# Polynomial-sketch attention and a gated FFN on one core: tokens in 64 rows of 17, sketches in 64x64 tiles, engines ordered by a list schedule

## The chip, the core and the metric

The kernel runs on one core of a Trainium2 chip. The core's engines are TensorE (PE in the profile; its weight loads are PEld), VectorE (DVE), ScalarE (ACT), GpSimd (POOL) and SyncE (SP), each with its own queue of instructions that it works through in order, and 16 DMA engines. The metric is the time of one execution on the device in microseconds; lower is better.

## What is computed

Four batches of four heads with 1088 tokens each and a head size of 32; the sketch size R is 8; the FFN takes 4352 tokens of width 128 (four heads side by side) through 1536 hidden columns.

```python
def phi(x):
    a = np.einsum('rd,bhsd->bhsr', S1, x)
    b = np.einsum('rd,bhsd->bhsr', S2, x)
    return np.einsum('bhsi,bhsj->bhsij', a, b).reshape(*x.shape[:-1], r * r)
q_p, k_p = (phi(q), phi(k))
kv = np.einsum('bhsf,bhsd->bhfd', k_p, v)
z = np.sum(k_p, axis=2)
num = np.einsum('bhsf,bhfd->bhsd', q_p, kv)
den = np.einsum('bhsf,bhf->bhs', q_p, z)[..., None] + 1e-06
attn = num / den
x = attn.transpose(0, 2, 1, 3).reshape(B * S, H * D)
out = np.maximum(x @ w_gate, 0.0) * (x @ w_val) @ w_out
```

A token of a head has 64 features, the outer product of its two sketches. Keys of a whole batch must be summed before a query of that batch can be finished.

## The kernel before, in words

**Tiling of tokens.** Of a batch's 1088 tokens the first 1024 lie as 128 partitions of 8 tokens (C = 8), in tiles k_sb, q_sb and v_sb with four heads along the free axis (load_main). The last 64 tokens of all four batches form a fifth group: kr, qr and vr, 32 partitions per batch with 2 tokens each (load_rest).

**Keys of a batch (class K).** t1 turns 32x32 blocks on VectorE (kt), so that the head dimension lies on the partitions, four heads at once. ab multiplies by the sketch matrix sk in fp32 on TensorE, 128 rows by 128 columns, 512 columns at a time. t2 turns the result back (abk). phi makes the outer products (kp) on POOL, for batch 0 half of them on VectorE. kvz sums kp times v and the sketches' products for z in one PSUM bank, four fp16 and one fp32 product per column of tokens, and then adds the leftover rows (abr, kpr, vr) with 32-row products. evac masks the sums into zd and kv_bd. w multiplies zd with s1rep and VectorE writes the result into wst, the matrix that queries are multiplied with; it yields both sketches and the denominator's factor.

**Queries (class Q).** Work goes in groups of n token columns: t1 (VectorE), ab (fp32 on TensorE, one product per head), t2 (VectorE), den (product on POOL or VectorE, sum and reciprocal on VectorE, scaling), phi (outer product qp), tr (2n transposes on TensorE), tre (copy to SBUF on ScalarE), num (two products with 64 columns each, one for each half of PSUM's partitions) and x (cast to xT on ScalarE). The groups are 2, 2 and 4 columns of batch 0, two of 4 for each other batch and 2 columns of leftover rows.

**FFN (class F).** 102 units, each of 512 columns: g (L414), Relu on ScalarE (L416), v (L419), product with v on VectorE to ht (L421), and four 128-column products of ht with wo into o_ps (L430), which gathers a group's output. The last unit of a group evicts o_ps on ScalarE (L437) and SyncE writes it out (L440, L447).

**Order.** manual_schedule keeps the written order on each engine. The head (L473 to L522) is written out by hand, with warm(n) putting n small products on zeros into TensorE's queue (L155, 111 in all). After it, at(slot, ...) puts attention steps into the loop over units (L565): keys some 46 to 11 units ahead of the batch's second group, queries 14 to 1.5 units ahead of their own. A unit's out comes LAG = 3 units behind its g and v, and 5 for a group's first.

**PSUM.** Two banks for g, three for v, one for o, two ("m") for all attention products. SBUF: four g_sb, eight ht.

**DMA.** SyncE issues k and q of each batch and the leftover rows; ScalarE issues S1, S2 and the leftover v; POOL issues v with a cast to fp16 and the three weight matrices, also with a cast.

Of the kernel before, what the change touches and what calls it, by code (L numbers as in the profile page):

```python
# [19 lines left out]
EPS = 1e-6  # L20


@with_exitstack
def kernel(
# [20 lines left out]
    C = S // 128  # L45
    SM = C * 128
    E = (S - SM) // 32
    GC = C // 2
    GT = GC * 128
    RT = E * 128  # L50
    LAG = 3
    HOLD = 2
    assert (B, H, D, R, S - SM) == (4, 4, 32, 8, 64)
# [4 lines left out]
    a_t = ctx.enter_context(tc.tile_pool(name="a_t", bufs=3))  # L58
    a_ab = ctx.enter_context(tc.tile_pool(name="a_ab", bufs=2))
    a_kp = ctx.enter_context(tc.tile_pool(name="a_kp", bufs=2))  # L60
    a_sm = ctx.enter_context(tc.tile_pool(name="a_sm", bufs=2))
    f_g = ctx.enter_context(tc.tile_pool(name="f_g", bufs=4))
    f_h = ctx.enter_context(tc.tile_pool(name="f_h", bufs=8))
    f_o = ctx.enter_context(tc.tile_pool(name="f_o", bufs=2))
    ps_g = ctx.enter_context(tc.tile_pool(name="ps_g", bufs=2, space=bass.MemoryType.PSUM))
    ps_v = ctx.enter_context(tc.tile_pool(name="ps_v", bufs=3, space=bass.MemoryType.PSUM))
    ps_o = ctx.enter_context(tc.tile_pool(name="ps_o", bufs=1, space=bass.MemoryType.PSUM))
    ps_m = ctx.enter_context(tc.tile_pool(name="ps_m", bufs=2, space=bass.MemoryType.PSUM))

    banks = {"m": ps_m, "g": ps_g, "v": ps_v}  # L70

    def bank(x="m"):
        return banks[x].tile([128, 512], FP32, name=f"{x}_ps")


    s16 = const.tile([2 * R, 4, D], FP32, name="s16")
    s1rep = const.tile([128, 4, D], FP32, name="s1rep")
    kr = const.tile([128, H, E * D], FP32, name="kr")
    qr = const.tile([128, H, E * D], FP32, name="qr")
    vr32 = const.tile([128, H, E * D], FP32, name="vr32")  # L80
    vr = const.tile([128, H, E * D], FP16, name="vr")
    k_sb = [const.tile([128, H, C * D], FP32, name=f"k_sb{b}") for b in range(B)]
    q_sb = [const.tile([128, H, C * D], FP32, name=f"q_sb{b}") for b in range(B)]
    v_sb = [const.tile([128, H, C * D], FP16, name=f"v_sb{b}") for b in range(B)]
# [4 lines left out]
    def load_main(eng, dst, src, b):  # L89
        eng.dma_start(out=dst, in_=src[b, :, 0:SM, :].rearrange("h (p c) d -> p h (c d)", c=C))  # L90

    def load_rest(eng, dst, src):
        for b in range(B):
            eng.dma_start(
                out=dst[32 * b:32 * b + 32],
                in_=src[b, :, SM:, :].rearrange("h (t e) d -> t h (e d)", e=E),
            )
# [3 lines left out]
    load_main(nc.sync, k_sb[0], k, 0)  # L101
    load_main(nc.gpsimd, v_sb[0], v, 0)
    load_rest(nc.sync, kr, k)
    load_rest(nc.scalar, vr32, v)
    load_main(nc.sync, q_sb[0], q, 0)
    for b in range(1, B):
        load_main(nc.sync, k_sb[b], k, b)
        load_main(nc.sync, q_sb[b], q, b)
    load_rest(nc.sync, qr, q)

# [3 lines left out]
    scr = const.tile([1, 1], FP16, name="scr")  # L114
    id32 = const.tile([2 * R, 2 * R], FP32, name="id32")
# [3 lines left out]
    nc.gpsimd.dma_start(out=wg, in_=moe_w_gate.rearrange("m (j f) -> m j f", j=NJ))  # L119
    nc.gpsimd.dma_start(out=wv, in_=moe_w_val.rearrange("m (j f) -> m j f", j=NJ))  # L120
    nc.gpsimd.dma_start(out=wo, in_=moe_w_out.rearrange("(j f) m -> f j m", f=128))
# [3 lines left out]
    maskz = const.tile([128, 2, H, R], FP32, name="maskz")  # L125
    nc.gpsimd.memset(maskz, 1.0)
    nc.gpsimd.affine_select(out=maskz, in_=maskz, compare_op=ALU.is_ge, fill=0.0, base=0,
                            pattern=[[-16, 2], [-32, H], [0, R]], channel_multiplier=1)
    nc.gpsimd.affine_select(out=maskz, in_=maskz, compare_op=ALU.is_ge, fill=0.0, base=R - 1,
                            pattern=[[16, 2], [32, H], [0, R]], channel_multiplier=-1)  # L130
    load_main(nc.gpsimd, v_sb[1], v, 1)
    mask = const.tile([128, 4], FP32, name="mask")
    maskw = const.tile([128, 4], FP32, name="maskw")
    maskkv = const.tile([128, 2, D], FP32, name="maskkv")
    sk = const.tile([128, 2, 4, 2, 2 * R], FP32, name="sk")
    wst = [const.tile([128, H, 4, 32], FP32, name=f"wst{b}") for b in range(B + 1)]
    bw = [const.tile([128, GC * H, R + 1], FP32, name=f"bw{i}") for i in range(2)]
    nc.vector.memset(mask, 0.0)
    nc.vector.memset(maskw, 0.0)
    nc.vector.memset(maskkv, 0.0)  # L140
    nc.vector.memset(sk, 0.0)
    for p in range(4):
        nc.vector.memset(mask[32 * p:32 * p + 32, p:p + 1], 1.0)
        nc.vector.memset(maskw[32 * p:32 * p + 32, p:p + 1], DSCALE)
# [3 lines left out]
    for i in range(2):  # L148
        nc.vector.memset(bw[i][:, :, R], EPS * DSCALE)

    def warm(n):

        ps = bank("v")
        for _ in range(n):
            nc.tensor.matmul(ps[:, 0:128], zero, zero, start=True, stop=True)  # L155

    nc.scalar.activation(out=scr, in_=zero[0:1, 0:1], func=ACTF.Relu)
    warm(42)
    st_ps = bank()
    nc.tensor.transpose(st_ps[:, 0:2 * R], s16.rearrange("f p d -> f (p d)"), id32)  # L160
    s_t = const.tile([128, 2 * R], FP32, name="s_t")
    nc.vector.tensor_copy(out=s_t, in_=st_ps[:, 0:2 * R])
    s1_ps = bank()
    nc.tensor.matmul(s1_ps[:, 0:128], sel.rearrange("r x f -> r (x f)"),
                     s16.rearrange("f p d -> f (p d)"), start=True, stop=True)
    nc.scalar.copy(out=s1rep.rearrange("p a d -> p (a d)"), in_=s1_ps[:, 0:128])
    warm(9)

    def fill_static(eng, w):
        eng.tensor_tensor(  # L170
            out=w[:, :, :, 0:2 * R],
            in0=s_t[:, None, None, :].to_broadcast([128, H, 4, 2 * R]),
            in1=mask[:, None, :, None].to_broadcast([128, H, 4, 2 * R]),
            op=ALU.mult,
        )

    for hf in range(2):
        nc.vector.tensor_tensor(
            out=sk[:, hf, :, hf, :],
            in0=s_t[:, None, :].to_broadcast([128, 4, 2 * R]),  # L180
            in1=mask[:, :, None].to_broadcast([128, 4, 2 * R]),
            op=ALU.mult,
        )


    kv_bd = [const.tile([128, 2, 2 * D], FP16, name=f"kv_bd{b}") for b in range(B)]
    xT = const.tile([HD, B * SM + RT], FP16, name="xT")
    abr = const.tile([128, E * H, 32], FP32, name="abr")
    kpr = const.tile([128, E * H, R * R], FP16, name="kpr")

    def outer(eng, dst, ab, a0, b0, n, a=None):

        a_src = ab[:, :, a0:a0 + R] if a is None else a
        eng.tensor_tensor(  # L194
            out=dst.rearrange("s x (i j) -> s x i j", i=R),
            in0=a_src[:, :, :, None].to_broadcast([128, n, R, R]),
            in1=ab[:, :, None, b0:b0 + R].to_broadcast([128, n, R, R]),
            op=ALU.mult,
        )

    def rest_k():
        kt = a_t.tile([128, E * H * 32], FP32, name="ktr")
        nc.vector.transpose(kt, kr.rearrange("p h (e d) -> p e h d", e=E))
        ps = bank("g")
        nc.tensor.matmul(ps[:, 0:E * H * 32], sk[:, 0].rearrange("p a b f -> p (a b f)"), kt,
                         start=True, stop=True)
        nc.vector.transpose(abr.rearrange("p x f -> p (x f)"), ps[:, 0:E * H * 32])
        outer(nc.gpsimd, kpr, abr, 0, R, E * H)

    class K:  # L210


        def __init__(self, b):
            self.b = b

        def t1(self, lo, n):

            if lo == 0:
                self.kt = a_t.tile([128, C, H, 32], FP32, name="kt")
            nc.vector.transpose(  # L220
                self.kt[:, lo:lo + n],
                k_sb[self.b][:, :, lo * D:(lo + n) * D].rearrange("p h (c d) -> p c h d", d=D))

        def ab(self, lo=0, n=GC, x="m"):

            self.ps = bank(x)
            for hf in range(2):
                nc.tensor.matmul(  # L228
                    self.ps[:, 0:n * 128], sk[:, hf].rearrange("p a b f -> p (a b f)"),
                    self.kt[:, hf * GC + lo:hf * GC + lo + n].rearrange("p c h t -> p (c h t)"),  # L230
                    start=(hf == 0), stop=(hf == 1))
# [13 lines left out]
        def kvz(self, lo=0, n=GC, rest=True, x="m"):  # L245
            b = self.b
            if lo == 0:
                self.m = bank(x)
# [20 lines left out]
            if not rest:  # L269
                return  # L270
# [309 lines left out]
    for u in pend:  # L580
        u.out()
# [31 lines left out]
```

## Time and profile before

| What | Value |
|---|---|
| Median of 3 runs | 136.78 us (135.47 to 140.0) |
| Span of the profiled execution | 133.8 us, 2942 instructions |
| The profiled execution's own time on the device | not given beside its span; the runs lie 1.7 to 6.2 us above the span, the median 3.0 |
| Busy: TensorE, VectorE, ScalarE, POOL | 116.8, 98.1, 76.8, 51.4 us |
| Mean granted TensorE clock | 0.995 |
| First g of the FFN; last product of TensorE | 22.69 us; ends at 129.2 us |
| Product to ht, Relu, fp32 key sketch of 512 columns (mean of one record) | 676, 602, 606 ns |
| HBM read and written | 9.05 and 2.23 MB |

How to read it: the span runs from the first to the last instruction of the execution. A row of the timeline gives start, duration, engine, line, operation, output and inputs, shapes, and how many instructions are joined in it. An fp32 product appears as two records. Durations of TensorE's products overlap, so the distance of two starts tells what one costs; the chain of waits goes back from the last instruction to whatever released each step.

### The profile page before, as it was taken

The page shows a single profiled execution, that of the slowest core. Times are in us where ns is not written, and L with a number is a line of the kernel's source. Part 1 is how long each engine was busy: PE and PEld are TensorE (multiplying, and loading weights), DVE is VectorE, ACT ScalarE, POOL GpSimd, SP SyncE. Part 2 cuts the span into 40 slices and gives each one's busy share as a digit, 9 for nine tenths or more (in the row PEclk, how much of TensorE's full clock was granted, in tenths as well). Part 3 has the DMA queues.
Part 4 walks back from the last instruction along what each step waited for, and adds up shares of the span by engine and source line. Part 5 has one row for each costly group of instructions (what it writes and reads, how often), then busy time and mean ns, then how long its engine had stood idle before and what let it go on. Part 6 is the DMA issues. An engine that isn't in the chain of part 4 may idle for free.

```text
span 133.8 us, 2942 instructions
## 1 busy us (share of the span) xinstructions
PE 116.8 (87%) x1102; PEld 82.8 (62%) x1102; DVE 98.1 (73%) x202; ACT 76.8 (57%) x136; POOL 51.4 (38%) x70
## 2 busy tenths in 40 slices
PE   6995989949989999699799998997999689999850
PEld 6984867739856665377466654765656356756740
DVE  4295578899768956997579649776895696988850
ACT  0311003747646674775576837845767949789930
POOL 6955307999602601980017018910260160050000
PEclk9999999999999999999999999999999999999998
DMA  2999999808501000200011002000200010020021
GB/s 63 255 208 253 270 257 355 235 1 105 91 5 39 0 2 0 78 5 0 0 50 34 0 0 83 5 0 0 77 2 5 15 66 0 0 83 0 0 78 39
DMA packets 11485, 9.23 MB, mean 69 GB/s; under 512 B 3792, under 2 KB 10320, under 8 KB 11472
## 3 DMA queue, kind: packets, MB, share of 16 engines
q1 hardware_dynamic: 6864, 6.69, 16.1%
q0 software_dynamic: 3952, 2.23, 11.8%
q10 hardware_dynamic: 656, 0.14, 0.6%
q8 instruction: 8, 0.13, 0.5%
q14 instruction: 5, 0.04, 0.1%
HBM read 9.05 MB, written 2.23 MB: 84 GB/s over the span
## 4 chain that ended last, share of the span: by engine, by line
PE 53%; DVE 15%; DMA 11%; POOL 7%; issue 6%; ACT 4%; ACTq 1%; DVEq 1%; SPq 0%; POOLq 0%
PE o_ps L430 12%; PE g_ps L414 11%; PE v_ps L419 10%; DMA k_sb<-in_k_dram 7%; DVE ht L421 7%; POOL qp L194 4%; PE m_ps L328 4%; PE m_ps L365 3%; DMA vr<-in_v_dram 3%; ACT g_sb L416 3%; PE m_ps L228 3%; DVE abq L336 2%; PE m_ps L264 2%; PE m_ps L383 2%; DVE kt L220 2%
## 5 line engine op out<-in xcount | busy, mean ns | idle before, releaser
L421 DVE TENSOR_TENSOR ht<-g_sb,v_ps 128x512 f16<-128x512 f16 x102 | 65.5, 676 | 16.9 <-ACT g_sb L416 9.4
L416 ACT ACTIVATE g_sb<-g_ps 128x512 f16<-128x512 f32 x102 | 59.5, 602 | 27.8 <-PE g_ps L414 26.5
L419 PE MATMUL v_ps<-xT,wv 128*128 128x512 f16 (+1 forms) x120 | 38.7, 347 | 4.6 <-DVE ht L421 4.6
L414 PE MATMUL g_ps<-xT,wg 128*128 128x512 f16 (+1 forms) x120 | 38.7, 347 | 1.9 <-ACT g_sb L416 1.8
L430 PEld LDWEIGHTS <-ht 128*128 128x128 f16 x408 | 28.7, 99 | 15.4 <-issue 4.4
L430 PE MATMUL o_ps<-wo,ht 128*128 128x128 f16 x408 | 36.2, 219 | 0.2 <-DVE ht L421 0.2
L343 POOL TENSOR_TENSOR bw<-abq 128x128 f32<-128x128 f32 (+1 forms) x7 | 3.0, 433 | 51.0 <-DVE abq L336 51.0
L194 POOL TENSOR_TENSOR qp<-an,abq 128x1024 f16<-128x1024 f32 (+2 forms) x10 | 16.7, 1669 | 7.4 <-DVE an L350 6.9
L419 PEld LDWEIGHTS <-wv 128*128 128x128 f16 x120 | 11.7, 98 | 7.9 <-issue 6.5
L194 POOL TENSOR_TENSOR kp<-abk 128x512 f16<-128x512 f32 x14 | 15.5, 1138 | 1.6 <-DVE abk L237 1.6
L373 ACT COPY pt<-m_ps 128x1024 f16<-128x1024 f16 (+1 forms) x10 | 8.8, 883 | 10.5 <-PE m_ps L365 10.2
L414 PEld LDWEIGHTS <-wg 128*128 128x128 f16 x120 | 11.2, 98 | 4.7 <-issue 3.0
L155 PE MATMUL v_ps<-zero 128*128 128x128 f16 x111 | 9.7, 255 | 1.1 <-DVE maskkv L140 1.1
L328 PE MATMUL m_ps<-qt,wst 128*128 128x128 f32 (+1 forms) x72 | 9.7, 277 | 0.6 <-DVE wst L300 0.6
L328 PEld LDWEIGHTS m_ps<-qt,wst 128*128 128x128 f32 x72 | 9.1, 192 | 1.4 <-DVE wst L300 0.8
L155 PEld LDWEIGHTS <-zero 128*128 128x128 f16 x111 | 8.6, 118 | 1.5 <-DVE maskkv L140 1.1
L437 ACT ACTIVATE o_sb<-o_ps 128x512 f32<-128x512 f32 (+1 forms) x10 | 5.3, 532 | 4.2 <-PE o_ps L430 4.2
L365 PEld LDWEIGHTS <-qp 128*128 128x128 f16 x68 | 4.4, 98 | 3.2 <-POOL qp L194 1.7
L336 DVE STREAM_TRANSPOSE abq<-m_ps 128x512 f32<-128x512 f32 (+1 forms) x9 | 5.9, 651 | 0.6 <-PE m_ps L328 0.6
L264 PE MATMUL m_ps<-abk 128*128 128x64 f32 x32 | 6.2, 289 | 0.0
L346 DVE TENSOR_REDUCE dn<-bw 128x16 f32<-128x144 f32 (+1 forms) x10 | 2.8, 281 | 4.5 <-POOL bw L343 4.4
L220 DVE STREAM_TRANSPOSE kt<-k_sb 128x512 f32<-128x512 f32 (+1 forms) x10 | 5.6, 576 | 0.6 <-DMA k_sb<-in_k_dram 0.6
(80 smaller groups left out, 100.4 us busy)
## 6 DMA issues: line engine op xcount, KB each, us to landing
k_sb<-in_k_dram SPq DMA_DIRECT2D x4, 512.0 KB, 10.0
q_sb<-in_q_dram SPq DMA_DIRECT2D x4, 512.0 KB, 12.2
out_dram<-o_sb SPq DMA_DIRECT2D x7, 256.0 KB, 2.0
v_sb<-in_v_dram POOLq DMA_DIRECT2D x4, 256.0 KB, 5.2
wg<-in_moe_w_gate_dram POOLq DMA_DIRECT2D x1, 384.0 KB, 6.2
wv<-in_moe_w_val_dram POOLq DMA_DIRECT2D x1, 384.0 KB, 7.7
wo<-in_moe_w_out_dram POOLq DMA_DIRECT2D x1, 384.0 KB, 15.0
out_dram<-o_sb SPq DMA_DIRECT2D x2, 128.0 KB, 1.8
```

What stands on the lines that cost most here:

```text
L155: nc.tensor.matmul(ps[:, 0:128], zero, zero, start=True, stop=True)
L194: eng.tensor_tensor(out=dst.rearrange("s x (i j) -> s x i j", i=R), in0=a_src[:, :, :, None].to_broadcast([128, n, R, R]), in1=ab[:, :, No ...
L264: nc.tensor.matmul(m[:, 128:192].rearrange("f (a h j) -> f a h j", a=2, h=H), ab.rearrange("s h f -> s (h f)"), ab.rearrange("s h (a f) -> ...
L328: nc.tensor.matmul(self.ps[:, h * n * 32:(h + 1) * n * 32], wst[self.b][:, h].rearrange("p a f -> p (a f)"), self.qt[:, :, h, :], start=Tr ...
L336: nc.vector.transpose(self.absb.rearrange("p (c h) f -> p c h f", h=H), self.ps[:, 0:n * 128].rearrange("p (h c t) -> p c h t", h=H, c=n))
L365: nc.tensor.transpose(self.ps[:, p, c], self.qp[:, c * H + 2 * p:c * H + 2 * p + 2].rearrange("s h f -> s (h f)"), ident)
L373: eng.copy(out=self.pt, in_=self.ps)
L414: nc.tensor.matmul(g_ps[:, y * W:(y + 1) * W], wg[:, j], x, start=True, stop=True)
L416: nc.scalar.activation(out=g_sb, in_=g_ps, func=ACTF.Relu)
L419: nc.tensor.matmul(v_ps[:, y * W:(y + 1) * W], wv[:, j], x, start=True, stop=True)
L421: nc.vector.tensor_tensor(out=self.ht, in0=g_sb, in1=v_ps, op=ALU.mult)
L430: nc.tensor.matmul(o[:, s], self.ht[:, y * W + s * 128:y * W + (s + 1) * 128], wo[:, j], start=(j == 0 and s == 0), stop=(j == NJ - 1), sk ...
```

## The change

The kernel body is written anew. What it computes, the FFN units and their number stay.

Tokens: a batch's 1088 tokens are 64 rows of 17. k and q lie with two heads on the partitions (128 = 2 heads x 64 rows) and two pairs of heads along the free axis; v lies as 64 rows of the first nine columns over 64 rows of the last eight. No group of leftover rows is loaded by itself; the ninth columns of all batches form the last query group. k of batch 0 comes in two loads by pair of heads, v of batch 0 over SyncE in fp32 with a cast on ScalarE.

Sketches: each product takes 64 rows (one head) and gives 64 partitions (one half of the columns), in four tiles; the two heads write to two adjoining PSUM banks. z is summed by itself, apart from kv. The numerator is one full-width product for each pair of heads, gathered in one bank.

Order: a plan (class Plan) holds every step with an engine, an assumed occupancy and latency, its dependencies, the banks it takes and frees, and due times worked back from the FFN units' (830 ns apart). At each step it takes, over all engines, the earliest task; among tasks of one engine within 30 ns the one due first. The order of planned starts is the order of issue. The assumed times fix only the order: no times are carried into the program. PSUM is one tile of eight banks: the out bank, up to five for g and v, three for attention once the FFN has started. There are ten g_sb, fourteen ht, four o_sb and five sets of query buffers. Filler products go before a TensorE task up to the first g, to three quarters of the planned gap.

```diff
-        eng.dma_start(out=dst, in_=src[b, :, 0:SM, :].rearrange("h (p c) d -> p h (c d)", c=C))
+    def load_pairs(eng, dst, src, b, hp=None):
+        x = src[b].rearrange("(x y) (t c) d -> (y t) x (c d)", y=2, c=C)
...
+    load_pairs(nc.sync, k_sb[0], k, 0, 0)
+    load_pairs(nc.sync, k_sb[0], k, 0, 1)
+    load_pairs(nc.sync, q_sb[0], q, 0)
+    load_v(nc.sync, v32, 0)
     for b in range(1, B):
+        load_pairs(nc.sync, k_sb[b], k, b)
+        load_pairs(nc.sync, q_sb[b], q, b)
...
+    P = Plan(free={"PE": 1200.0, "ACT": 3000.0, "DVE": 2600.0, "POOL": 3600.0},
+             a_max=3, f_max=5, n_banks=7)
...
+        def ke_ab(t, b, hp, first):
+            for h2 in range(2):
+                for st in range(2):
+                    r = slice(64 * h2, 64 * h2 + 64)
+                    nc.tensor.matmul(
+                        ps[64 * st:64 * st + 64, first.bank + h2, 0:CA * 32],
+                        sk[r, hp].rearrange("p a b f -> p (a b f)"),
+                        kt[b][r, hp, CA * st:CA * st + CA].rearrange("p c t -> p (c t)"),
+                        start=hp == 0, stop=hp == 1, skip_group_check=True)
+
+        first = P.add(f"k{b}ab0", "PE", 650, 900, deps=[K.t1[0], t_sk], banks=2)
...
+        def ke_z(t, b):
+            for c in range(CA):
+                x = c % 2
+                ab = abk[b][:, c].rearrange("p h f -> p (h f)")
+                nc.tensor.matmul(ps[64 * x:64 * x + 64, t.bank, 0:H * R], ab,
+                                 ab.rearrange("p (h f) -> p h f", h=H)[:, :, R:2 * R],
+                                 start=c < 2, stop=c >= CA - 2, skip_group_check=True)
...
+        def ke_kv(t, b, lo, hi, m):
+            for c in range(lo, hi):
+                for hp in range(2):
+                    nc.tensor.matmul(
+                        ps[:, m.bank, hp * 64:hp * 64 + 64], kp[b][:, hp, c],
+                        v_sb[b][:, 2 * hp:2 * hp + 2, c * D:(c + 1) * D],
+                        start=(lo == 0 and c == 0 and hp == 0), stop=c == CA - 1,
+                        skip_group_check=True)
...
+        def qe_ab(t, G):
+            n = G.n
+            for hp in range(2):
+                for h2 in range(2):
+                    r = slice(64 * h2, 64 * h2 + 64)
+                    for st in range(2):
+                        o = ps[64 * st:64 * st + 64, t.bank + h2, hp * n * 32:(hp + 1) * n * 32]
...
+                            nc.tensor.matmul(o, wst[G.bs[0]][r, hp].rearrange("p a f -> p (a f)"),
+                                             G.qt[r, hp, st].rearrange("p c t -> p (c t)"),
...
+                    nc.tensor.matmul(
+                        o, kv_bd[G.bs[0]][:, 2 * hp:2 * hp + 2].rearrange("f a d -> f (a d)"),
+                        G.pt[:, hp].rearrange("f c t -> f (c t)"), start=hp == 0, stop=hp == 1)
...
+    T0, STEP = 13000.0, 830.0
...
+            g = P.add(f"g{u}", "PE", 218, 218 + 170, deps=[G.x], banks=1, kind="f",
+                      emit=lambda t, f=e_mm: f(t, wg), at=land["w"] - 3000.0)
...
+            o = P.add(f"out{u}", "PE", 230, 230 + 170, kind="f",
+                      deps=[mult, last_evict if i == 0 else None, outs[-1] if outs else None],
+                      emit=lambda t, U=U, f=e_out: f(t, U), at=land["w"])
...
+            n = int((t.start - now) * 0.75 / (107.0 if now < 5000.0 else 57.0))
+            for _ in range(n):
+                nc.tensor.matmul(ps[:, OB, 0:128], zero, zero, start=True, stop=True)
```

The first query group's den and phi run on VectorE, those of all others on POOL. Key phi runs on POOL, for batch 0's last five columns on VectorE.

## The prediction

> **What bounds the kernel now.** I read the busy table first, then the timeline of TensorE in steady state, the chain of waits, and the timelines of the head and of the end.
>
> ```profile
> PE 116.8 (87%) x1102; PEld 82.8 (62%) x1102; DVE 98.1 (73%) x202; ACT 76.8 (57%) x136; POOL 51.4 (38%) x70
> PEclk9999999999999999999999999999999999999998
> ```
> TensorE is the fullest engine, at a granted clock of 0.9 to 1.0 in all slices, so pace and not clock is the question. Its busy time has modelled ends; the pace is read from starts. TensorE's rows of the steady stretch, by start and duration:
>
> ```profile
> 73.36 0.38 PE L414 MATMUL g_ps<-xT,wg 128*128 128x512 f16 x1
> 73.58 0.38 PE L419 MATMUL v_ps<-xT,wv 128*128 128x512 f16 x1
> 73.79 0.39 PE L430 MATMUL o_ps<-wo,ht 128*128 128x128 f16 x4
> 74.02 0.38 PE L414 MATMUL g_ps<-xT,wg 128*128 128x512 f16 x1
> 74.23 0.38 PE L419 MATMUL v_ps<-xT,wv 128*128 128x512 f16 x1
> 74.54 0.41 PE L383 MATMUL m_ps<-pt,kv_bd 128*64 128x512 f16 x2
> 74.88 0.40 PE L430 MATMUL o_ps<-wo,ht 128*128 128x128 f16 x4
> ```
> From g at 73.36 to the next g at 74.02 an FFN unit costs TensorE 0.655 us (three times 0.218). VectorE does six products in 3.73 us (0.61 each) and ScalarE two Relus in 1.25 us, so TensorE leads narrowly. 102 units make 66.8 us.
>
> The first g stands at 22.69 us and TensorE ends at 129.2: a stretch of 106.5 us. The attention work in it, by starts: key sketches 2 x 1.77; key sums 3 x 2.2 (1.45 for the main rows, 0.75 with its gap for the leftover rows); the w product 3 x 0.44; query sketches 7 x 0.95 + 0.84; transposes 64 x 0.055; numerators 7 x 0.43 + 0.6. That is 26.0 us. So 66.8 + 26.0 = 92.8 us is work and 13.7 us is waiting: about 3 us per batch (a batch takes 26.5 to 27), some 2.5 us near 27 to 30 us where v waits for ht, 2 at the end.
>
> The head is a chain, not an engine:
>
> ```profile
> 6.32 9.98 DMA k_sb<-in_k_dram
> 16.32 0.71 DVE kt L220
> 17.26 1.10 PE m_ps L328 x8
> ```
> The next batch's keys landed at 16.3 us; VectorE waited for them with the write of wst queued behind. Before that the key sums had waited for the leftover rows, whose small loads took SyncE 4.5 us to issue ahead of q0. After TensorE's end come 4.5 us: last eviction, output write, closing (129.3 to 133.8).
>
> **The head, part by part.** The leftover-row work goes: its loads from three queues, the transposes, the sketch, kpr on POOL, wrest. S reaches s_t at 6.0 us now because 42 filler matmuls stand ahead; fewer do so later (their number comes from planned gaps; a filler costs 0.055 and only where it outlasts the gap). k0 needed 4.4 us to land, so both halves should be in by 6. Then, from rows of nearest shape: second half transposed (544 columns, 0.72 by 0.69 for 512) 6.9; sketch 0.8 plus drain 0.2, 7.9; two transposes back at 0.45 to 0.5, 8.9; z 1.2, 10.1; mask 0.22, w 0.5, wst 0.28, 11.2; q0 sketch 0.8, 12.0; transpose 0.45, 12.5; four VectorE steps of 0.25, 13.5; two outer products of 0.43 on VectorE (POOL's 0.87 leaves this path), 14.3; transposes and copy 0.4 + 0.6, 15.3; numerator 0.3 and xT 0.4: first g at 16.2, against 22.69. wst no longer needs phi, v or the leftover rows; that is most of the gain. v0 comes over SyncE's queue in fp32 and ScalarE casts it in two copies (about 1.1 each by the 1.01 copy of 1024); ScalarE is idle there, and cover lasts until the numerator at 15.3. If v0 lands after 12 the chain pays the difference.
>
> DMA: the bytes read are the same, k and q in runs of 17 tokens instead of 8. The weights' issues on POOL move behind the masks and ring memsets, some 1.1 us later than 2.9 to 4.0. wo landed 15 us after its issue; now 19 to 20.5. g and v need only wg and wv (6.2 and 7.7 us after issue). The out products are queued in TensorE's order behind three or four units and everything on TensorE behind them; I take 1.5 us of stall, between 0 and 3. POOL's v loads (0.8 per issue, two per batch) sit in its idle 62%. Memsets of wst, kt, v_sb and kv_bd cost POOL about 1 us per batch (0.53 for 512 columns), in the same idle time; without that cover they would delay the first phi of the next keys.
>
> **The stretch.** FFN: 102 units before and after, 66.8. Attention on TensorE, each from a row:
>
> Key sketch: eight 64x64 products of 288 columns per batch, in two visits. An fp32 matmul is two records, and 512 columns take 0.443 per record, so 288 take 0.249. If the four tiles of a visit run together: 0.50 + 0.1 for the first loads + 0.2 for entering and leaving = 0.8. One after another: 8 x 0.249 + 0.2 = 2.2. Query sketch, full group: eight products of 128 columns, 16 records. Whole-width fp32 loads pace 0.117 per record (8 records with 64 columns in 0.94); half the columns, 0.059. So 16 x 0.059 + 0.2 = 1.14; all tiles together would be 0.64, none 1.98.
>
> The nearest row for tiles is the numerator, two column halves:
>
> ```profile
> 122.38 0.33 PE L388 MATMUL m_ps<-pt,kv_bd 128*64 128x64 f16 x8
> 122.64 0.23 PEld L430 LDWEIGHTS <-ht 128*128 128x128 f16 x4
> ```
> Eight loads and products in 0.26 us, 0.033 each; and above, two of 512 columns from 74.54 to 74.88, 0.34 where 0.43 would be serial. Before that row 0.09 us is idle (74.23 + 0.218 to 74.54), and 0.34 is 0.12 more than one product. So column halves overlap, and a visit costs about 0.2. No row shows two row halves together; I take overlap, as for columns, and keep the serial price for a rival. z: 18 records x 0.059 + 0.2 = 1.26 (0.7 to 2.3). w as before, 0.44. kv: 18 x 0.031 = 0.56 (four took 0.12). Numerator: two full-width products, 0.43, no visit. Last group: 32 records, 2.1.
>
> Sum: 6 x 0.8 + 3 x (1.26 + 0.44 + 0.56) + 7 x 1.14 + 2.1 + transposes 3.5 + numerators 3.5 = 28.7 us, against 26.0. TensorE gains no time; it loses 2.7, and K1's sketch, in the head before, is now counted here. Work: 66.8 + 28.7 = 95.5.
>
> The Trainium skill, "TensorE: Matmul & The Clock Gate", Part 3, says that a weight load overlaps running matmuls only where its row group differs. That speaks against this change, whose two token halves share rows. The eight-in-0.26 row speaks for overlap within one row group. By the rule a key visit would be 2 x 2 x (0.249 + 0.059) + 0.2 = 1.43 and a query sketch 1.56, together some 7 us more and a time near 132. I go by the row. "TensorEngine Tiling (Array Packing)", Tiling Modes, also says that a change of tiling mode drains the engine; the row gives 0.2 per visit, and 20 visits are 4.0 us already in the sum, which would be 4.0 lower if no drain were paid.
>
> Other engines over the same stretch: VectorE 102 x 0.61 = 62 + keys 3 x 3.0 + queries 7 x 1.75 + 1.4 = 85 us; ScalarE 102 x 0.5 to 0.6 + groups 7 x 1.9 = 64 to 75; POOL less than half. TensorE still leads by about 10 us.
>
> Waits: a list schedule places each engine's work when its inputs should be there, with up to five FFN banks, ten g and fourteen ht buffers. Today's waits sit at zd (0.8), at v for ht (up to 1.4) and at numerators behind late chains; starting attention earlier and letting FFN run ahead removes such waits. I take 3.0 in three and a half batches, 1.5 at wo and 1.5 at the end: 6.0, between 3 and 15. Each wait holds all that TensorE has queued.
>
> Span: 16.2 + 95.5 + 6.0 + 4.5 = 122.2. The profiled span of 133.8 stands 3.0 below the median 136.78 of the runs, which go from 135.47 to 140.0; the same on top gives 125.2 us.
>
> **Rivals.** (B) The waits stay: in-order queues built from estimated costs stall as often as today, 13.7 plus 1.5 at wo. For it: VectorE has only 10 us of slack. Against: deeper buffers. 16.2 + 95.5 + 15.2 + 4.5 + 3.0 = 134.4. (C) The other side: tiles run one after another. Key visits +1.4 x 6, query sketches +0.84 x 7, head +2.2: 16.5 more, 141.7 us. For it: no row has row halves together. Against: the column rows above. It makes the kernel slower than today from 11.6 us of excess on, some 70% serial. (D) The head doesn't shorten, because v0 or the weights come late in a DMA that is 90% busy from 3 to 25 us: first g at 22.7, 131.7 us. Against: k and v0 are ahead on their queue. (E) Four tiles truly together and few waits: query sketches 0.64 (8 x 0.5 less), z 0.7 (3 x 0.56 less), so TensorE 89.8, waits 3.5: 117.0.
>
> **How the numbers follow.** Forecast 0.50, B 0.16, C 0.17, D 0.07, E 0.10. Two per cent, about what a measurement of this kernel tells from none, is 134.0 to 139.5. Faster: 0.50 + 0.10 + 0.07 of B (which stands on the bound) + 0.05 of D = 0.72; same: 0.08 of B, 0.02 of D, 0.02 of C = 0.12; slower: 0.15 of C and 0.01 of B = 0.16. The forecast's own range is 118 to 130; 115 to 138 leaves out about 0.04 below and 0.16 above.
>
> **What would show it.** First g near 16 us and no wait of wst for k1. Query sketches spaced 1.1 us per group in the starts, 0.8 per key visit; 2.0 and 2.2 would be C. wo landing near 20 with TensorE idle until then by 1 to 2 us. Idle of TensorE after the first g of about 6 us; near 14 is B. I am wrong if VectorE or POOL, not TensorE, releases most waits, or if the FFN unit is no longer 0.655.

## The result, and the profile after

The changed kernel takes 123.39 us (median of four runs, 121.62 to 123.96). The kernel before, run beside it on the same chip, takes 138.12 us (135.47 to 140.0). The ratio is 0.9008, with a 95% interval of 0.8823 to 0.9193: faster, and inside the range of the prediction. It leaves out executions in a second, slower state (of the changed kernel it keeps 121.62 and 123.32 us), so it is not the quotient of the two medians. The profiled execution has a span of 121.6 us against 133.8, so 12.2 us have gone.

The page of the changed kernel, its busy line and TensorE's two rows in 40 slices:

```profile
PE 106.3 (87%) x1248; PEld 71.2 (59%) x1248; DVE 94.5 (78%) x203; ACT 78.6 (65%) x137; POOL 50.7 (42%) x89
PE   4599687339999999999999999999999999999910
PEclk9999999976999999999999999999999999999995
```
From the tenth slice to the thirty-eighth TensorE is busy nine tenths or more of the time. The 33 in slices eight and nine is a hole, and the granted clock falls in slices nine and ten. The waits of TensorE say what ends the hole (engine, line, releaser: us in total, times, longest):

```profile
PE ps L717 <- DMA wo<-in_moe_w_out_dram: 4.2, 1, 4.2
PE ps L320 <- DMA s<-in_S_dram: 1.9, 1, 1.9
PE ps L566 <- DVE wst L461: 1.1, 1, 1.1
```
The out products (L717) wait 4.2 us for wo. The chain of waits runs through the same transfer (start, us, what):

```profile
3.10 0.67 POOL wg L364
3.76 0.53 POOL wv L364
4.30 22.08 DMA wo<-in_moe_w_out_dram
26.42 0.58 PE ps L717 x4
```
wo is issued at 4.3 us and lands at 26.4. In the kernel before it took 15.0 us from issue to landing. Three stretches of the changed kernel (from:to, length, then busy us and instructions of PE, PEld, DVE, ACT, POOL, then granted clock, DMA share, GB/s):

```profile
19.31:26.42 7.11, 2.31 (x21) 1.71 (x20) 3.73 (x6) 2.99 (x6) 5.43 (x7) 0.96 1.28 252
26.42:31.50 5.08, 5.08 (x44) 4.24 (x44) 1.98 (x3) 3.11 (x6) 0.00 (x0) 0.72 0.36 47
31.50:110.00 78.50, 78.46 (x908) 50.02 (x905) 71.86 (x137) 62.65 (x110) 32.76 (x39) 1.00 0.11 25
```
From the first g (19.31) until wo lands, TensorE works 2.3 of 7.1 us. Then it works without a gap at a granted clock of 0.72. After that it is busy for 78.46 of 78.5 us. The kernel before, in the same window:

```profile
sum 78.50, PE 72.46 PEld 47.78 DVE 60.28 ACT 52.30 POOL 29.59; mean PE 24.15 PEld 15.93 DVE 20.09 ACT 17.43 POOL 9.86
```
Its 6.0 us of idle time are gone. TensorE's steady rows of the changed kernel, with the new products between FFN units:

```profile
42.42 0.38 PE L686 MATMUL ps<-xT,wg 128*128 128x512 f16 x1
42.73 0.67 PE L566 MATMUL ps<-qt,wst 64*64 64x128 f32 x16
43.33 0.40 PE L717 MATMUL ps<-wo,ht 128*128 128x128 f16 x4
...
45.45 0.77 PE L442 MATMUL ps<-abk 128*64 128x32 f32 x18
46.15 0.40 PE L717 MATMUL ps<-wo,ht 128*128 128x128 f16 x4
```
A query sketch takes 0.60 us from start to start (42.73 to 43.33), z takes 0.70 (45.45 to 46.15). A key visit takes 0.65. In front of each that follows an FFN product stands a gap of about 0.09: the g at 42.42 costs 0.22 of the 0.31 us to the next start.

Where the 12.2 us came from: the first g stands at 19.31 instead of 22.69 (3.4 less). From there to TensorE's end it is 96.9 us instead of 106.5 (9.6 less). The rest after TensorE is 5.4 instead of 4.6 us (0.8 more). Of the 96.9 us some 88.0 are work: 66.8 for the FFN units as before, and about 21 for attention, by starts and with the gaps in front. Some 9 are waits and slow pace: 4.8 of idle time until wo has landed, about 1.4 in the slow stretch behind it (5.1 us for work that costs 3.7 at the steady pace) and about 1.2 at the end are the largest parts. Before, it was 92.8 and 13.7. So work gave about 4.8 us and waiting about 4.8.

### The profile page after: what moved, and what is told of

Read it like the earlier page. It is cut to its first block, busy times and chain, and to the rows that moved or that the text cites. A ratio compares the mean times of both kernels' runs of the same rounds, so it can differ in the third digit from the quotient of the medians.

```text
span 121.6 us, 3214 instructions
## 1 busy us (share of the span) xinstructions
PE 106.3 (87%) x1248; PEld 71.2 (59%) x1248; DVE 94.5 (78%) x203; ACT 78.6 (65%) x137; POOL 50.7 (42%) x89
## 3 DMA queue, kind: packets, MB, share of 16 engines
q1 hardware_dynamic: 4496, 7.24, 21.2%
q0 software_dynamic: 3472, 2.02, 11.7%
HBM read 9.05 MB, written 2.23 MB: 93 GB/s over the span
## 4 chain that ended last, share of the span: by engine, by line
PE 73%; DMA 18%; POOL 3%; DVEq 1%; issue 0%; DVE 0%; ACT 0%; POOLq 0%
PE ps L686 37%; PE ps L717 20%; DMA wo<-in_moe_w_out_dram 18%; PE ps L399 3%; PE ps L627 3%; PE ps L566 3%; PE ps L643 3%; PE ps L442 2%; PE ps L483 1%; PE ps L453 1%; POOL wg L364 1%; PE ps L571 1%; DVEq L790 0%; POOL wv L364 0%; DVE ht L706 0%
## 5 line engine op out<-in xcount | busy, mean ns | idle before, releaser
L706 DVE TENSOR_TENSOR ht<-g_sb,ps 128x512 f16<-128x512 f16 x102 | 65.8, 680 | 13.5 <-ACT g_sb L697 5.2
L697 ACT ACTIVATE g_sb<-ps 128x512 f16<-128x512 f32 x102 | 58.4, 604 | 11.8 <-PE ps L686 9.4
L717 PE MATMUL ps<-wo,ht 128*128 128x128 f16 x408 | 39.8, 220 | 4.6 <-DMA wo<-in_moe_w_out_dram 4.2
L717 PEld LDWEIGHTS <-ht 128*128 128x128 f16 x408 | 30.1, 98 | 22.9 <-issue 5.4
L686 PE MATMUL ps<-xT,wv 128*128 128x512 f16 (+1 forms) x120 | 37.7, 351 | 0.0
L686 PE MATMUL ps<-xT,wg 128*128 128x512 f16 (+1 forms) x120 | 37.3, 352 | 0.0
L287 POOL TENSOR_TENSOR kp<-abk 128x512 f16<-128x512 f32 (+1 forms) x14 | 15.9, 1159 | 18.3 <-DVE abk L411 18.3
L633 ACT COPY pt<-ps 128x1024 f16<-128x1024 f16 (+1 forms) x10 | 8.9, 886 | 13.7 <-PE ps L627 13.7
L287 POOL TENSOR_TENSOR qp<-an,abq 128x512 f16<-128x512 f32 x16 | 16.7, 1068 | 0.4
L686 PEld LDWEIGHTS <-wg 128*128 128x128 f16 x120 | 11.3, 99 | 2.8 <-issue 1.2
L686 PEld LDWEIGHTS <-wv 128*128 128x128 f16 x120 | 11.4, 99 | 1.7 <-issue 0.3
L760 PE MATMUL ps<-zero 128*128 128x128 f16 x103 | 8.8, 239 | 1.1 <-DVE zero L238 1.1
L399 PE MATMUL ps<-kt,sk 64*64 64x288 f32 x64 | 6.7, 494 | 0.0
## 6 DMA issues: line engine op xcount, KB each, us to landing
q_sb<-in_q_dram SPq DMA_DIRECT2D x4, 544.0 KB, 11.7
k_sb<-in_k_dram SPq DMA_DIRECT2D x3, 544.0 KB, 13.6
wv<-in_moe_w_val_dram POOLq DMA_DIRECT2D x1, 384.0 KB, 10.5
wo<-in_moe_w_out_dram POOLq DMA_DIRECT2D x1, 384.0 KB, 22.1
```

The lines of the kernel that those rows point to most:

```text
L287: eng.tensor_tensor(out=dst.rearrange("s x (i j) -> s x i j", i=R), in0=a[:, :, :, None].to_broadcast([128, n, R, R]), in1=b[:, :, None, : ...
L399: nc.tensor.matmul(ps[64 * st:64 * st + 64, first.bank + h2, 0:CA * 32], sk[r, hp].rearrange("p a b f -> p (a b f)"), kt[b][r, hp, CA * st ...
L633: emit=lambda t, G=G, f=tr: nc.scalar.copy(out=G.pt.rearrange("f p c t -> f (p c t)"), in_=ps[:, f.bank].bitcast(FP16)[:, 0:2 * G.n * 128]))
L686: nc.tensor.matmul(ps[:, t.bank, y * W:(y + 1) * W], w[:, j], xT[:, G.col:G.col + W], start=True, stop=True)
L697: nc.scalar.activation(out=U.g_sb, in_=ps[:, g.bank], func=ACTF.Relu)
L706: nc.vector.tensor_tensor(out=U.ht, in0=U.g_sb, in1=ps[:, vv.bank], op=ALU.mult)
```

## The experiments

The theory after the result: the list order removes TensorE's waits; the 64x64 tiles run beside each other and so make attention cheaper; what is left is the wait for wo. The rivals: the deeper rings of g and ht removed the waits, or the new layout by itself did; the row halves of a tile do not overlap; wo is late for a reason other than k and q. In the experiments the kernel before took 135.7 to 136.6 us (medians) when it ran beside them. In e3_full_rows, e7_head and e9_head2 the sketches of batch 3's keys are partly read from a PSUM bank that a later query product has already taken over, because the plan places the second of the two transposes first and frees the banks with it; their instructions and their work are the full ones.

**e1_late_k.** k and q of batches 2 and 3 go to ScalarE's queue and are issued later.

```diff
-    for b in range(1, B):
-        load_pairs(nc.sync, k_sb[b], k, b)
-        load_pairs(nc.sync, q_sb[b], q, b)
+    load_pairs(nc.sync, k_sb[1], k, 1)
+    load_pairs(nc.sync, q_sb[1], q, 1)
...
+    for b in range(2, B):
+        for nm, dst, src in (("k", k_sb[b], k), ("q", q_sb[b], q)):
+            P.add(f"ld_{nm}{b}", "ACT", 550, 550, at=14500.0, emit=lambda t, dst=dst, src=src, b=b:
+                  load_pairs(nc.scalar, dst, src, b))
```


> Keys and queries of batches 2 and 3 are loaded from ScalarE's queue after the casts of v0, in place of SyncE's queue at the start. Theory (wo landed at 26.4 us because SyncE's queue holds all of k and q and shares the DMA engines with the weights): bytes ahead of wo fall from about 7 to 5.1 MB, so wo lands near 18 to 20; TensorE's wait of 4.2 us for it goes to below 1, and the half-speed pace that follows it (granted clock 0.72 from 26.4 to 31.5 us, some 1.4 us) goes too: 5 to 6 us less, 117 to 119 us. Rival (wo's own queue on POOL takes 22 us whatever else is loaded): wo still lands at 25 or later and the time stays at 123 plus or minus 1.5.

Measured: 118.91 us (118.88 to 118.99), ratio 0.8747 [0.8684, 0.881]. The profile's DMA issues (KB each, us from issue to landing):

```profile
wo<-in_moe_w_out_dram POOLq DMA_DIRECT2D x1, 384.0 KB, 16.6
```
TensorE no longer waits for wo, and the granted clock stays at 0.9 and more in all slices but the end. The transfer was late because SyncE had k and q of all batches in flight next to it: its queue carried 7.24 MB over the whole span against 5.02 here, the written output of 2.23 included in both. The wait and the slow stretch behind it together are worth 3.5 us by the two ratios (0.9008 and 0.8747) and 4.5 by the medians, with a first g that stands 1.5 us later here (20.78).

**e2_rings.** `NG = 4` and `NH = 8`, as many g_sb and ht as before, instead of 10 and 14.

> The rings go back to the sizes of before: 4 tiles g_sb and 8 ht in place of 10 and 14; the plan is made anew for them. Theory (deep rings are what took the 13.7 us of TensorE's waits away): waits return, TensorE idle between 31.5 us and its end by 4 to 10 us, 127 to 133 us. Rival (the list order did it, by starting attention early; the rings add nothing): idle below 1 us in that stretch, time within 1.5 us of 123.4.

Measured: 123.34 us (121.87 to 125.54), ratio 0.8968 [0.8864, 0.9071]; span 120.0, TensorE busy for 78.45 of the 78.5 us from 31.5 on. The deep rings bring nothing. This reason, which the prediction gave against its rival B, falls.

**e3_full_rows.** The key sketches multiply all 128 rows, with zeros for the other head, so that tiles of different rows cannot run at the same time.

```diff
-                        sk[r, hp].rearrange("p a b f -> p (a b f)"),
-                        kt[b][r, hp, CA * st:CA * st + CA].rearrange("p c t -> p (c t)"),
+                        sk2[:, h2, hp],
+                        kt[b][:, hp, CA * st:CA * st + CA].rearrange("p c t -> p (c t)"),
```


> The key sketches use all 128 rows: the weights of each head are padded with zeros over the other head's rows, so two products of a visit can no longer run in two row halves; columns stay halved. The number of products and their columns stays; a constant scale of the denominator is 1 in place of 1/16. Theory (all four tiles of a visit run together: 2 records of 0.249 us plus 0.15): a visit goes from 0.65 to about 1.15 us, six visits in the stretch after 31.5 us add 3.0 us, the head 0.5 to 1: 126.5 to 127.5. Rival (row halves already run one after another and only column halves overlap): visits stay at 0.65 us, no change.

Measured: 128.37 us (126.58 to 130.02), ratio 0.934 [0.9225, 0.9455]. TensorE's rows:

```profile
43.95 1.19 PE L408 MATMUL ps<-kt,sk 128*64 128x288 f32 x8
45.08 0.40 PE L726 MATMUL ps<-wo,ht 128*128 128x128 f16 x4
```
A visit takes 1.13 us instead of 0.65, so the row halves do run side by side. The time grew by 5.0 us by the medians and 4.5 by the ratios, more than eight visits of 0.48 explain (3.8); the median lies above the theory's range. The plan still counted 650 ns for a visit. e11_rows_planned takes that up.

**e4_tile_order.** The loops over column half and row half change places in both sketches.

```diff
-            for h2 in range(2):
-                for st in range(2):
+            for st in range(2):
+                for h2 in range(2):
```


> The two innermost loops of key and query sketches are swapped, so that neighbouring products differ in their rows (row half alternates) instead of sharing them. Theory (loads of 64 columns overlap in either order): key visits stay at 0.65 and query visits at 0.60 us, within 0.04, time within 1 us. Rival (a weight load overlaps only with a product in other rows, and the present order pays for it): query visits fall to 0.45 us or lower, 10 visits save 1.5 us or more.

Measured: 123.98 us in a single execution, span 122.3; key visits 0.64 to 0.65, query sketches 0.60, as before the edit. The order of tiles does not show in these rows. The Trainium skill, "TensorE: Matmul & The Clock Gate", Part 3, lets a weight load overlap running products only where the row group differs; loads that follow each other within one row group are as quick here, so this case does not show that rule.

**e5_hand_order.** From the first g on, the tasks of the new layout are sorted into the order of the kernel before (units with slots, keys 46 to 11.5 units ahead, queries 14 or 25 to 1.5, out three units behind), and the banks are split as there: two for g, three for v, two for attention.

```diff
+    rest.sort(key=lambda t: (slot(t), place[id(t)]))
...
+                own = {"g": (0, 1), "v": (2, 3, 4), "a": (5, 6)}[kind]
```


> The changed kernel with the order of before: up to the first g the planned order stays; after it every step stands in the slot, counted in FFN units, that the kernel before gives it (out three units behind g and v, keys 46 to 11 units and queries 25 to 1.5 units ahead), and banks go as before: two for g, three for v, two for attention. Tiles, layout, rings and loads are those of the changed kernel. Theory, since smaller rings changed nothing: the list order itself took the waits away, so TensorE idles again by 8 to 13 us after the first outs, 130 to 137 us. Rival (the new layout did it: shorter visits, z apart from kv, no leftover rows): idle below 3 us there, 122 to 126.5 us.

Measured: 138.13 us (136.41 to 138.72), ratio 1.0103 [1.0004, 1.0202]. The windows from 31.5 to 110 us, summed:

```profile
sum 78.50, PE 65.11 PEld 40.98 DVE 58.35 ACT 51.21 POOL 25.34; mean PE 21.70 PEld 13.66 DVE 19.45 ACT 17.07 POOL 8.45
```
The program's work is the same, but TensorE idles 13.4 us there instead of 0.04, a little more than the theory's 8 to 13. Its waits in the whole span, besides 4.1 us for wo, are led by

```profile
PE ps L442 <- DVE kv_bd L498: 4.3, 3, 1.6
PE ps L399 <- DVE abq L582: 3.3, 2, 1.7
PE ps L686 <- DVE ht L706: 3.2, 4, 1.4
```
z (L442) and the key sketches (L399) do not read kv_bd or abq: they wait for the banks that these VectorE steps free. The whole gain hangs on the order and the banks. The lead times were those of the old layout and were not fitted to the new one, so this is an upper bound of what the plan is worth.

**e6_flat_costs.** The list order stays, but the plan counts 400 ns occupancy and 500 ns latency for every step of ScalarE, VectorE and POOL whose cost followed from its size.

```diff
-        return dict(occ=50 + 0.835 * n, lat=175 + 0.835 * n)
+        return dict(occ=400, lat=500)
```


> The plan is made with wrong costs: every step on ScalarE, VectorE and POOL is taken to occupy 400 ns and to be done after 500, whatever its size; TensorE's costs stay. Theory (the order is good because the assumed times are close to the measured ones): steps of POOL that take 1.1 to 2 us come late, TensorE waits 4 us or more in the steady stretch, 127 to 135 us. Rival (due times and dependencies are enough; the exact costs hardly matter): within 1.5 us of 123.4.

Measured: 135.18 us (134.41 to 136.56), ratio 0.9909 [0.9831, 0.9988]. The same summed windows:

```profile
sum 78.50, PE 71.78 PEld 45.89 DVE 63.54 ACT 56.54 POOL 33.05; mean PE 23.93 PEld 15.30 DVE 21.18 ACT 18.85 POOL 11.02
```
6.7 of the 11.5 us by which the span grows are idle time in these windows; waits for ht are the largest (4.6 in the whole span). The rest lies before and after them. The time stands just above the theory's 127 to 135. Made from these flat times, the list order is no better than the order written by hand (138.13 us above, 133.02 in e8_hand_shared).

**e8_hand_shared.** As e5_hand_order, with all seven banks open to everyone; the one that has been free longest is taken.

> As the hand-ordered kernel, but every product takes the bank of the seven that has been free longest, so that no step waits for a bank of its own kind; the order of the steps on each engine is the same hand order. Theory (the order itself makes the waits): the waits for a bank (4.3 us of z for kv_bd and 3.3 us of key sketches for abq in the hand-ordered run) move to ht and g_sb or go down by less than half; 130 us or more. Rival (the fixed split of banks made them): TensorE's waits fall by 7 us or more, 128 us or less.

Measured: 133.02 us (132.56 to 135.22), ratio 0.9774 [0.9651, 0.9896], span 131.0. The summed windows:

```profile
sum 78.50, PE 67.78 PEld 41.66 DVE 59.82 ACT 51.97 POOL 26.78; mean PE 22.59 PEld 13.89 DVE 19.94 ACT 17.32 POOL 8.93
```
Against e5_hand_order the span is 5.4 us shorter: 2.7 in these windows (67.78 less 65.11) and 2.9 because the wait for wo falls from 4.1 to 1.2. The time fits the theory (130 us or more), but the waits for banks have not gone down; they have moved to the products of the FFN:

```profile
PE ps L686 <- DVE kv_bd L498: 4.9, 3, 1.8
PE ps L686 <- DVE abk L411: 3.3, 3, 1.3
```
g and v (L686) read neither kv_bd nor abk, so these are waits for banks. They come from the hand order, which keeps attention's banks long, or from the simple rule by which a bank is taken here; the runs do not tell these apart. So the other 10.7 us (from 67.78 to 78.46) belong to the plan's order and its choice of banks together, and opening the banks alone gives back the smaller part.

**e7_head.** Three edits: k and q of all batches but the first go to ScalarE's queue (planned at 10.5 and 14.5 us), batch 0's outer products all go to POOL, and 17 more fillers stand in front of S.

```diff
-                on_dve = b == 0 and i == 1
+                on_dve = False
...
+            n += 17 * (now == 1200.0)
```


> Three edits of the head: keys and queries of batches 1 to 3 are loaded from ScalarE's queue after v0's casts; all of batch 0's key products run on POOL, so that wst is not queued behind two products of 1.2 us on VectorE; 17 more filler products stand in front. Theory (the head is a chain and TensorE is never idle behind it): wo lands near 17 to 18.5, the key visits of the head run at 0.65 in place of 1.17 us, first g at 16 to 17 in place of 19.3, 114.5 to 117 us. Rival (with wo early the head's chain is covered: only the amount of work after the first out counts): 118 to 119, as with late loads alone.

Measured: 116.12 us (116.03 to 117.76), ratio 0.8557 [0.848, 0.8634]. wst is written at 11.7 instead of 13.55 us, wo lands 14.6 us after its issue. The time is in the theory's range, but two of its steps did not come: the key visits of the head still take 1.17 us each, and the first g stands at 18.8, not at 16 to 17.

**e9_head2.** Late loads as in e7_head, but batch 0's second outer products stay on VectorE, now behind wst.

```diff
+        if b == 0:
+            for hp in range(2):
+                K.phi[4, hp].deps.append(K.wst)
```


> Keys and queries of batches 1 to 3 come from ScalarE's queue as in the head experiment, batch 0's last key products stay on VectorE but are made to depend on wst, so that wst goes first; no extra fillers. Theory (wst behind two products of 1.2 us on VectorE was the head's lost 2.4 us, late loads the other 4.5): wst at about 11.8 us, first g at 17 to 18.5, wo at 19 or earlier, 115 to 117 us. Rival (the two products only move onto the query chain behind them): first g at 19 or later, 117 to 119 us.

Measured: 118.69 us (118.57 to 118.77), ratio 0.8726 [0.8666, 0.8787]. wst is written at 12.3, but the first g stands at 20.75, as in e1_late_k (20.78), not at 18.8 as in e7_head. The rival had it so. The products now stand in front of the query steps on VectorE, and TensorE waits 1.7 us for VectorE's qp. They have to leave VectorE, not only wst's path.

**e10_head_safe.** e7_head with one dependency more, so that a sketch's banks cannot be freed between its two transposes.

```diff
-            K.t2.append(P.add(f"k{b}t2{lo}", "DVE", **dve((hi - lo) * 64, 110), deps=[second],
+            K.t2.append(P.add(f"k{b}t2{lo}", "DVE", **dve((hi - lo) * 64, 110), deps=[second] + K.t2,
```


> This is e7_head with one more dependency in the plan: the second transpose of a batch's sketches waits for the first one, so that the banks which their common second task frees can't be given away before both are written. Theory (the time of e7_head came from the late loads and the early key products, and not from a bank that was given away too soon): the same work in nearly the same order, 115.5 to 117.0 us beside e7_head's 116.12. Rival (the bank given away early was part of the gain): key transposes wait and push the attention of batches 2 and 3 back, 117.5 us or more.

Measured: 117.04 us (116.2 to 118.19), ratio 0.8574 [0.847, 0.8677]. The ratio is within e7_head's interval: the theory holds, with the median just above its range of 115.5 to 117.0, and the bank given away early was no visible part of the gain. This version beats both kernels of the study.

**e11_rows_planned.** e3_full_rows with the plan told of longer visits (1150 and 1400 ns instead of 650 and 900) and the dependency of e10_head_safe.

> Key sketches with full 128 rows (padded with zeros, so that no two tiles with different rows can overlap), as in e3_full_rows, but with the plan told of the longer visits (1150 ns instead of 650) and the same extra dependency as e10_head_safe. Theory (the two row halves of a 64x64 visit run beside each other, which is worth 0.48 us a visit): six visits in the steady part give 2.9 us and the two of the head 0.5 to 1, so 126.5 to 127.5 us beside 123.4. Rival (the excess of 5 us of e3_full_rows was the plan's wrong cost, and the overlap of the halves is hidden): 125 us or less.

Measured: 125.12 us (124.49 to 125.33), ratio 0.918 [0.9118, 0.9242]; span 123.0, 1.4 over the changed kernel's. That is between the theory and its rival. The key sketches' group has 11.3 us busy instead of 6.7, 4.6 more, so the overlap of the row halves is real. But the wait for wo shrinks from 4.2 to 2.3 and that for wst (1.1) goes: longer visits early on fill time in which TensorE waited anyway. e3_full_rows is longer than this run by 3.2 us by the medians and 2.2 by the ratios. What parts the two is the planned times and the dependency; e10_head_safe shows no cost of the dependency, so most of it goes with the plan's wrong times.

**e12_more_fillers.** e10_head_safe with 42 fillers in front of S instead of 29.

> e10_head_safe with 13 more filler products in front of S, 42 in all, as many as the kernel before had. There TensorE had reached its full pace by 6.4 us (fillers of 0.073), while in e7_head and e10_head_safe, with 29 fillers, the key visits at 6 to 9 us still took 1.17 us instead of 0.65. Theory (the pace goes up after 4 to 5 us of whole-array products without a gap): 42 fillers last until 5.7, S is 1.0 us later, the two key visits then cost 0.65 each, wst is written where it was (within 0.3 of 12.2) and the time stays at 116.5 to 117.5 us. Rival (the pace goes up only after the first visits, whatever stands ahead): visits stay at 1.17, wst comes 1 us later and the time is 117.5 to 118.5 us.

Measured: 118.49 us (117.3 to 119.32), ratio 0.8755 [0.869, 0.882]. The head on TensorE in e10_head_safe, then in this run:

```profile
1.06 3.27 PE L764 MATMUL ps<-zero 128*128 128x128 f16 x29 [1.06 <-DVE zero L235]
...
6.42 1.24 PE L402 MATMUL ps<-kt,sk 64*64 64x288 f32 x8
7.59 0.50 PE L764 MATMUL ps<-zero 128*128 128x128 f16 x3
```

```profile
1.06 4.50 PE L764 MATMUL ps<-zero 128*128 128x128 f16 x42 [1.06 <-DVE zero L235]
...
6.72 0.72 PE L402 MATMUL ps<-kt,sk 64*64 64x288 f32 x8
7.37 0.34 PE L764 MATMUL ps<-zero 128*128 128x128 f16 x3
```
A visit takes 0.65 us here (6.72 to 7.37) and 1.17 there. wst comes at 11.2 instead of 12.2 and the first g at 18.1 instead of 19.0. So the theory of the pace held in the rows, better than expected, since S's own products were quicker too. The time did not fall: the median lies in the rival's range, and the two fastest executions took 117.3 and 117.8 us against 116.2 and 116.25 in e10_head_safe. Only one execution of each has a profile, the longest of e10_head_safe (span 116.5 us, two others 114.5) and the shortest of this run (115.6, others up to 117.5). The pace in the others is not known, and why the earlier head does not show in the times stays open.

## Why the prediction was right, and where its terms were off

The forecast of 125.2 stands 1.8 us above the measured 123.39, but errors of both signs cancel in it: that it came so close is luck. Against the span before, the prediction had the head 6.5 us shorter, the waits 7.7 less and TensorE's work 2.7 more; measured were 3.4, 4.8 and 4.8 less. That head and waits would bring a gain was right; that work would bring another was not foreseen.

- **The visits were priced too high.** By starts in the stretch, prediction against profile: key sketches 4.8 and 3.9, query sketches of full groups 8.0 and 3.6 (six of them), the last group 2.1 and 0.6, z 3.8 and 2.1, w 1.3 and 0.7; kv, transposes and numerators about as forecast. In all attention took some 21 us, not 28.7. The step that failed is "16 x 0.059 + 0.2 = 1.14": it took weight loads of 64 columns as half of a full-width load, one after another. The 0.64 of rival E was right for a query sketch (0.60). e3_full_rows shows for the key sketch that the four tiles run together; for the query sketch only the price shows it. The plan in the kernel counted 650 ns for a key visit, where the prediction's sum took 0.8 us. "TensorE gains no time; it loses 2.7" is wrong; it gains about 4.8. Of the "20 visits" only 17 carry 0.2 us in the sum, 3.4 us and not 4.0, and the gap in front of one measures 0.09.
- **The head was priced too low.** The first g was forecast at 16.2 and stands at 19.3. VectorE's rows of the head:

```profile
9.92 1.32 DVE L547 STREAM_TRANSPOSE qt<-q_sb 128x256 f32<-128x256 f32 x3
11.17 0.15 DVE L448 TENSOR_TENSOR zd<-ps,maskz 128x32 f32<-128x32 f32 x1
11.24 2.38 DVE L287 TENSOR_TENSOR kp<-abk 128x640 f16<-128x640 f32 x2
13.55 0.18 DVE L461 TENSOR_TENSOR wst<-ps,maskw 128x32 f32<-128x32 f32 x1
```
  wst does not need the outer products kp, as the prediction said, but two of them, 1.2 us each, stand ahead of it in VectorE's queue; the prediction left the queue out. wst comes at 13.6 instead of 11.2. The queue is some 1.9 us of that: in e7_head, where nothing stands ahead of wst and the key visits are just as slow, it comes at 11.7. The key visits at half pace (1.17 each instead of 0.65) cost about 1 us, as e12_more_fillers shows, and a cheaper z (0.70 instead of 1.2) takes half of it back. The last 0.8 us lie between wst and the first g, where the transposes of the next two query groups (0.44 and 0.67 us, from 14.94 on) stand between the first group's steps on VectorE.
- **wo was late by more than forecast.** "wo landing near 20" and 1.5 us of stall became 26.4 and 4.2, with slow products for 5 us behind it. The prediction moved wo by its own queue (POOL) and counted equal bytes; it did not ask how much SyncE would have in flight beside it once the small loads of leftover rows no longer held SyncE back. SyncE's last issue of q, before and after:

```profile
15.37 3.36 SPq L90 DMA_DIRECT2D q_sb<-in_q_dram  x1
8.80 2.93 SPq L218 DMA_DIRECT2D q_sb<-in_q_dram  x1
```
  e1_late_k shows that the early k and q are the cause.
- **The batches have no waits, where 3.0 were forecast.** Between 31.5 and 110 us there is no idle time; what is left besides wo stands before 22 us and in the last 6 us. The reason given, "starting attention earlier and letting FFN run ahead", is right, but not by "deeper buffers" (e2_rings): it is the plan's order together with its choice of banks (e5_hand_order), with fair assumed times (e6_flat_costs); what each of the two is worth by itself stays open (e8_hand_shared). Rival B, whose queues stall as often as before, is what e6_flat_costs and e5_hand_order look like.
- **FFN, tail.** The unit stays at 0.655; the tail is 5.4 instead of 4.5.

The sum: work in the stretch 88.0 instead of 95.5 (7.5 less), head 3.1 more, waits 8.9 instead of 6.0 (2.9 more), tail 0.9 more. That is 0.6 less, a span of 121.6 instead of 122.2. The median stands 1.8 above the span, not 3.0, which is the other 1.2 us. The prediction's 3.0 set the span of one execution against the median of others; in the runs here an execution mostly takes 1.7 to 2.2 us more than its own span.

## What to carry to other kernels

On in-order engines a list order with its choice of banks can remove waits that deeper buffers do not touch, but only with times that fit: flat costs gave nearly all of it back (135.2 us). When small loads leave a queue, ask what the queue will now put in flight earlier, and who shares the DMA engines with it; a weight that is needed late can become the longest wait. When pricing a chain's step, read the engine's queue in front of it as well as its inputs.

## What the runs showed of the hardware

- Four fp32 products (eight records) of 64 rows on 64 columns with 288 columns of data take 0.65 us in four tiles, and 1.13 us when each product takes all 128 rows (e3_full_rows). The order of the tiles made no difference in the one execution of e4_tile_order. About 0.09 us are lost in front of a visit that follows a full-width product.
- TensorE ran at half pace for 8 us or more of the head, while the row of granted clocks shows 0.9 or more there: a filler product took 0.11 us, later 0.055. In the profile of e12_more_fillers, after 42 fillers without a gap (4.4 us), all that followed ran at full pace; in those of e7_head and e10_head_safe, after 29 (3.2 us), followed by products of 16 rows and 64x64 tiles with hardly a gap, it did not until after 9 us. The Trainium skill, "TensorE: Matmul & The Clock Gate", Part 1, gives some 3.4 us of sustained work for this; 3.2 and 4.4 us lie on either side of it, but no run here shows the threshold itself. After the wait of 4.2 us for wo the granted clock was 0.72 over 5.1 us.
- The same 384 KB of wo took 15.0, 22.1, 16.6 and 14.6 us from issue to landing in the kernel before, the changed one, e1_late_k and e7_head; the seven other runs with the changed kernel's loads lie at 21.1 to 23.1. The late k and q are what e1_late_k changes. The Trainium skill, "DMA: Bandwidth & Descriptors", section "Queues, rings and completion order", says that a DMA engine goes round between the queues that have work, packet by packet; these numbers fit that, but no run here shows the turns themselves.
